# The first batch's attention output is split into the first token block's operands directly instead of through memory

## The chip, the core and the metric

The kernel runs on one core of one Trainium2 chip. The metric is the device time of one execution in microseconds (us). The kernel before takes 888.13 us, the median of three runs (887.55 to 888.17).

A core has five engines that run their own instruction streams and wait for one another by semaphores: TensorE (PE; matrix products and transposes into PSUM, PEld is its weight load), VectorE (DVE), ScalarE (ACT), GpSimd (POOL) and SyncE (SP), which here issues most of the DMAs.

## The reference

All arrays are fp32. `q`, `k` and `v` are 4 batches x 8 heads x 576 tokens x 64. The attention output becomes `x`, 2304 tokens x 512, and goes through two feed-forward stages:

```python
q_d, k_d, v_d = means over groups of 4 tokens          # 144 tokens per head
out_up = repeat(softmax(q_d k_d^T / 8) v_d, 4)          # pooled attention
mask = |i - j| < 4
out_local = softmax(where(mask, q k^T / 8, -1e6)) v     # local attention
x = (out_up + out_local) as (2304, 512)

h = x @ w_in                                            # 512 x 2048
x = (h * sigmoid(1.702 h)) @ w_out                      # 2048 x 512
y = ((x @ w1) * (x @ w2)) @ w3 @ w_out2                 # 512x1024, 512x1024, 1024x1024, 1024x512
```

## The kernel before

**Numbers.** A product in fp32 precision is made of three TensorE products (`mm3`, L117 to L120). Each operand is first split in two (`split`, L113): ScalarE copies it, rounded, into the high part `hi` (L114), and another engine subtracts that from the original to get the low part `lo` (L115). The weights come from memory in a packed form of two 32-bit words per number. Such a tile `st` of 512 KB is loaded, ScalarE makes `dec` from one word (L166), VectorE puts in the rest in three instructions (`decode`: L173, L176, L179), and then the tile is split into `w` (L184).

**Stage 0 (to about 120 us).** Nothing in the last two products lies between `w3` and `w_out2`, so they are folded into one matrix first, `w34 = w3 @ w_out2`, in 16 steps: 2 halves x 8 column tiles `j`. A step transposes a `w3` tile on TensorE (`w34_transpose`, L568, into `ps_w`, then split into `w3t`) and multiplies it (`w34_mm`, L578). After the eighth step of a half four results leave PSUM as `w34s` (L585, L586) and are written to memory. Between the products, `pump()` puts pieces of the first batch's attention: four head pairs, each with its transposes (`t_piece`, `qT` and `kT`, and the pooled `qd`, `kd`), local and pooled scores (`s_local` `ps_s`, `s_pool` `ps_sp`), softmax (`el`, `ep`), its transposes (`p_piece`, `ps_pt`) and values (`v_pool`, and `v_local` twice). The later `v_local` call of a pair covers the last 256 of the 576 tokens, the earlier one the first 320.

**How x gets to block 0.** `v_local` (L415 to L432) adds the local and the pooled part on VectorE into `xo` (L426) and writes it to the array `x_d` in memory (L430). When stage 0 is issued, `tok_load` (L593) loads 512 tokens of one head pair from there into `xr`, and `tok_split` (L598) splits it into `x_t`, for each of the four pairs (`kk`).

**Token blocks.** The feed-forward stage goes over blocks of 512, 512, 512, 256 and 512 tokens. In a block, step `f` of 16 makes 128 columns of `h` (`h_step`, L614: four `mm3`, one for each pair `kk`) and adds its share of `y` (`y_step`, L631); two `h` steps run ahead of their `y` step. The first block also carries the second batch's attention between its products, and the weights for each step are loaded, decoded and split just ahead of it.

**Memory on the chip.** Tiles live in pools with tags; a tile waits until an earlier tile of its tag is no longer read. The weight pool `wp` has 32 slots of tag "w". In `g2p` the tag "ys" has two slots, shared by `xo`, `w34s` and the block results. Staging tiles (`stage_tile`, L125) come from `stp` with three slots; in stage 0, four of each seven come from `xp`, whose four tags `x0` to `x3` later hold `x_t`.

**Order.** Each engine runs its instructions in one fixed order. The framework's scheduler makes it at build time, from the code's order, the dependencies and priorities (`decode` and the side work raise theirs). SyncE's DMA issues stand in such an order too: one that waits for its tile holds the ones behind it.

Of the kernel before, what the change touches and what calls it, by code (L numbers as in the profile page):

```python
# [10 lines left out]
F32R = mybir.dt.float32r  # L11
I32 = mybir.dt.int32
# [8 lines left out]
def fused_kernel(ctx, tc, q, k, v, w_in, w_out1, w1, w2, w3, w_out2, out):  # L21
    nc = tc.nc
    B, H, S, D = q.shape
# [6 lines left out]
    KD = DM // 128  # L30
# [4 lines left out]
    QB = 64  # L35
# [19 lines left out]
    NB = 512  # L55
# [9 lines left out]
    wp = ctx.enter_context(tc.tile_pool(name="wp", bufs=2 * NF))  # L65
    stp = ctx.enter_context(tc.tile_pool(name="stp", bufs=3))
    dp = ctx.enter_context(tc.tile_pool(name="dp", bufs=2))
    xp = ctx.enter_context(tc.tile_pool(name="xp", bufs=1))
# [10 lines left out]
    x_d = dram.tile([128, KD, NT], F32, name="x_d")  # L79
# [30 lines left out]
    def f32(ap):  # L110
        return ap.bitcast(F32)

    def split(raw, hi, lo, lo_eng):  # L113
        nc.scalar.activation(hi, raw, AF.Copy)  # L114
        lo_eng.tensor_tensor(lo, raw, f32(hi), op=ALU.subtract)  # L115
# [9 lines left out]
    def stage_tile(first):  # L125

        i = early["st"]
        early["st"] += 1
        if first and i % (3 + KD) >= 3:
            return xp.tile([128, 512, 2], I32, tag=f"x{i % (3 + KD) - 3}", name="st")  # L130
        return stp.tile([128, 512, 2], I32, tag="st", name="st")

    def decode_tile(first):
# [13 lines left out]
    def load_rows(w, f, first=False):  # L147
        st = stage_tile(first)
        nc.sync.dma_start(out=st.rearrange("p e w -> p (e w)"), in_=w.bitcast(I32)[f * 128:(f + 1) * 128, :])
        return st  # L150
# [73 lines left out]
            del self.decoded[:n]  # L224


    at = {}

    def head_ap(src, b, hp, tok, dims):
        off = ((b * H + 2 * hp) * S + tok) * D  # L230
# [184 lines left out]
    def v_local(n, i0, i1):  # L415
        vw, od = at["vw", n, i0 // HQ], at["od", n]
        xo = g2p.tile([128, NB], F32, tag="ys", name="xo")[:, :(i1 - i0) * QB]
        ps = pst.tile([128, (i1 - i0) * QB], F32, tag="t", name="ps_v")
        for i in range(i0, i1):
            for h in range(2):  # L420
                p = slice(h * D, (h + 1) * D)
                nc.tensor.matmul(
                    ps[p, (i - i0) * QB:(i - i0 + 1) * QB], vw[:, i - i0, h], at["PT", n, i // NPH][:, i % NPH, h * QB:(h + 1) * QB],
                    start=True, stop=True)
        u0, u1 = i0 * UB, i1 * UB
        nc.vector.tensor_tensor(  # L426
            xo.rearrange("p (u r) -> p u r", r=FAC), ps.rearrange("p (u r) -> p u r", r=FAC),
            od[:, u0:u1].unsqueeze(2).to_broadcast([128, u1 - u0, FAC]), op=ALU.add)
        b, hp = divmod(n, HP)
        nc.sync.dma_start(out=x_d[:, hp, b * S + i0 * QB:b * S + i1 * QB], in_=xo)  # L430
        if i1 == NQB and n + 1 < B * HP and n + 1 not in LOCAL:
            att_load_v(n + 1)  # L432

# [154 lines left out]
            pump()  # L588


    xh, xl, xr = {}, {}, {}

    def tok_load(src, j, kk):  # L593
        c0, n = BLOCKS[j]
        xr[j, kk] = t = g2p.tile([128, NB], F32, tag="xr", name="xr")
        nc.sync.dma_start(out=t[:, :n], in_=src[:, kk, c0:c0 + n])

    def tok_split(j, kk):  # L598
        n = BLOCKS[j][1]
        t = xr.pop((j, kk))  # L600
        x = xp.tile([128, 2, NB], F32R, tag=f"x{kk}", name="x_t")
        xh[kk], xl[kk] = x[:, 0], x[:, 1]
        split(t[:, :n], xh[kk][:, :n], xl[kk][:, :n], nc.vector)

    def tok_rest(src, j):
        for kk in range(KD):
            tok_split(j, kk)
            if kk + 2 < KD:
                tok_load(src, j, kk + 2)
# [172 lines left out]
    if True:  # L782
# [50 lines left out]
            jobs.size(njobs(s + 4))  # L833
        pump.drain()
        early["pri"] = 100
        tok_load(x_d, 0, 0)
        tok_load(x_d, 0, 1)
        jobs.split(2)
        tok_rest(x_d, 0)

        def w34_load(f):
            t = g2p.tile([128, NB], F32, tag="xr", name="w34r")
# [143 lines left out]
```

## Time and profile before

| | |
|---|---|
| median of three runs | 888.13 us |
| the profiled execution | 892.31 us |
| its span, first to last instruction | 890.5 us |
| TensorE busy, mean granted clock | 846.0 us (95%), 0.986 |
| VectorE busy | 589.5 us (66%) |
| ScalarE busy | 408.7 us (46%) |
| GpSimd busy | 150.6 us (17%) |
| bytes moved | 150.76 MB, 169 GB/s |

The profiled execution is one run with the profiler on; its span is 1.8 us shorter than its time. In the profile a line like `PE L118 MATMUL ps_h<-x_t,w` is an instruction of line 118 that writes the tile `ps_h` and reads `x_t` and `w`; `[0.63 <-DVE x_t L115]` behind it says that the engine was idle for 0.63 us before it, and what released it. PEclk is the granted TensorE clock as a share of full speed.

### The profile page before, as it was taken

How to read it: one execution, taken by the hardware profiler on the slowest of the kernel's cores; microseconds unless marked ns; L12 is line 12 of the kernel's file. 1: busy time of each engine (PE TensorE's matmuls, PEld its weight loads, DVE VectorE, ACT ScalarE, POOL GpSimd, SP SyncE). 2: the span in 40 equal slices, each digit the busy share in tenths (PEclk: the TensorE clock that was granted, in tenths of full speed). 3: DMA queues.
4: the chain of work that ended last, by engine and by line, in shares of the span. 5: the costliest groups of instructions: out<-in, count | busy, mean ns of one | idle time of the engine just before them, and what ended most of it. 6: DMA issues, size and time to landing. Idle time of an engine off the chain costs nothing.

```text
span 890.5 us, 13711 instructions
## 1 busy us (share of the span) xinstructions
PE 846.0 (95%) x5132; PEld 712.1 (80%) x5132; DVE 589.5 (66%) x1053; ACT 408.7 (46%) x862; POOL 150.6 (17%) x153
## 2 busy tenths in 40 slices
PE   5789979999999999999999999999999999999998
PEld 4567757666677777777789988889999899989996
DVE  5997587889998795847758973253456455555551
ACT  4667567567657665455446663342112211232111
POOL 7524241244332323311200000000000000000000
PEclk9799999999999999999999999999999999999999
DMA  8865584565656243553348989102556364635521
GB/s 239 270 207 160 155 249 129 163 182 170 158 156 123 63 108 87 131 126 62 78 148 304 358 325 348 49 1 86 210 196 259 105 244 166 255 135 222 191 84 71
DMA packets 140598, 150.76 MB, mean 169 GB/s; under 512 B 86898, under 2 KB 121460, under 8 KB 136436
## 3 DMA queue, kind: packets, MB, share of 16 engines
q1 hardware_dynamic: 119424, 141.21, 49.1%
q10 hardware_dynamic: 21108, 8.69, 4.0%
q8 instruction: 40, 0.66, 0.3%
q14 instruction: 26, 0.21, 0.1%
HBM read 117.75 MB, written 32.11 MB: 168 GB/s over the span
## 4 chain that ended last, share of the span: by engine, by line
PE 72%; DVE 12%; DMA 7%; issue 3%; ACT 3%; POOL 2%; ACTq 0%; SPq 0%; DVEq 0%; POOLq 0%
PE ps_ab L120 7%; PE ps_ab L118 7%; PE ps_ab L119 7%; PE ps_h L118 6%; PE ps_y L118 5%; PE ps_y L120 5%; PE ps_h L119 5%; PE ps_y L119 5%; PE ps_h L120 5%; PE ps_o L120 4%; PE ps_o L119 4%; PE ps_o L118 4%; DMA st<-in_moe_w_in_dram 3%; DVE dec L179 2%; DVE st L176 2%
## 5 line engine op out<-in xcount | busy, mean ns | idle before, releaser
L118 PE MATMUL ps_h<-x_t,w 128*128 128x512 f32 (+1 forms) x320 | 122.7, 385 | 3.0 <-DVE w L115 2.0
L118 PE MATMUL ps_y<-gh,w 128*128 128x512 f32 (+1 forms) x320 | 122.5, 383 | 0.0
L119 PE MATMUL ps_h<-x_t,w 128*128 128x512 f32 (+1 forms) x320 | 119.2, 372 | 1.1 <-DVE x_t L115 1.1
L119 PE MATMUL ps_y<-gl,w 128*128 128x512 f32 (+1 forms) x320 | 118.8, 371 | 0.4 <-DVE gl L115 0.4
L120 PE MATMUL ps_y<-gh,w 128*128 128x512 f32 (+1 forms) x320 | 119.2, 372 | 0.0
L120 PE MATMUL ps_h<-x_t,w 128*128 128x512 f32 (+1 forms) x320 | 118.5, 370 | 0.0
L120 PE MATMUL ps_ab<-b_t,a_in 128*128 128x384 f32 x336 | 112.5, 335 | 0.0
L118 PE MATMUL ps_ab<-b_t,a_in 128*128 128x384 f32 x336 | 112.5, 335 | 0.0
L119 PE MATMUL ps_ab<-b_t,a_in 128*128 128x384 f32 x336 | 112.4, 334 | 0.0
L115 DVE TENSOR_TENSOR gl<-g_t,gh 128x512 fp32r<-128x512 f32 (+1 forms) x80 | 55.0, 690 | 65.8 <-ACT gh L114 65.5
L624 ACT ACTIVATE g_t<-ps_h 128x512 f32<-128x512 f32 (+1 forms) x80 | 44.3, 555 | 92.0 <-PE ps_h L120 87.9
L114 ACT ACTIVATE abh<-ab 128x384 fp32r<-128x384 f32 x24 | 12.7, 527 | 137.5 <-DVE ab L749 137.5
L118 PEld LDWEIGHTS ps_h<-x_t,w 128*128 128x128 f32 x320 | 60.5, 190 | 17.2 <-DVE w L115 3.7
L118 PEld LDWEIGHTS ps_y<-gh,w 128*128 128x128 f32 x320 | 60.5, 189 | 11.8 <-issue 2.4
L119 PEld LDWEIGHTS ps_h<-x_t,w 128*128 128x128 f32 x320 | 60.8, 190 | 11.0 <-DVE x_t L115 2.2
L120 PEld LDWEIGHTS ps_y<-gh,w 128*128 128x128 f32 x320 | 60.5, 189 | 10.4
L120 PEld LDWEIGHTS ps_h<-x_t,w 128*128 128x128 f32 x320 | 60.5, 189 | 10.4 <-issue 0.2
L119 PEld LDWEIGHTS ps_y<-gl,w 128*128 128x128 f32 x320 | 60.6, 189 | 9.3 <-DVE gl L115 0.5
L118 PEld LDWEIGHTS ps_ab<-b_t,a_in 128*128 128x128 f32 x336 | 63.1, 188 | 0.9
L119 PEld LDWEIGHTS ps_ab<-b_t,a_in 128*128 128x128 f32 x336 | 63.1, 188 | 0.9
L179 DVE SCALAR_TENSOR_TENSOR dec<-dec,st 128x512 int32<-128x512 int32 x72 | 59.3, 833 | 6.0 <-ACT dec L166 4.8
L120 PEld LDWEIGHTS ps_ab<-b_t,a_in 128*128 128x128 f32 x336 | 63.1, 188 | 0.0
(150 smaller groups left out, 1667.3 us busy)
## 6 DMA issues: line engine op xcount, KB each, us to landing
a_in<-a_d SPq DMA_DIRECT2D x24, 1792.0 KB
st<-in_moe_w_dram SPq DMA_DIRECT2D x32, 512.0 KB
a_d<-ap SPq DMA_DIRECT2D x8, 1792.0 KB
st<-in_moe_w_out_dram SPq DMA_DIRECT2D x24, 512.0 KB
st<-in_moe_w_in_dram SPq DMA_DIRECT2D x16, 512.0 KB
yr<-y_d SPq DMA_DIRECT2D x12, 384.0 KB
out_dram<-osb SPq DMA_DIRECT2D x17, 256.0 KB
s_v<-in_v_dram ACTq DMA_DIRECT2D x15, 288.0 KB
```

Source lines behind the costliest of these rows:

```text
L114: nc.scalar.activation(hi, raw, AF.Copy)
L115: lo_eng.tensor_tensor(lo, raw, f32(hi), op=ALU.subtract)
L118: nc.tensor.matmul(ps, ll, rh, start=start, stop=False, skip_group_check=more)
L119: nc.tensor.matmul(ps, lh, rl, start=False, stop=False, skip_group_check=more)
L120: nc.tensor.matmul(ps, lh, rh, start=False, stop=stop, skip_group_check=more)
L176: nc.vector.scalar_tensor_tensor(low, st[:, :, 1], -0x80000000, low, op0=ALU.bitwise_and, op1=ALU.bitwise_or)
L179: nc.vector.scalar_tensor_tensor(t, t, 3, st[:, :, 0], op0=ALU.logical_shift_left, op1=ALU.bitwise_or)
L624: nc.scalar.activation(g[:, :n], ps[:, :n], AF.Gelu_apprx_sigmoid)
```

## The change

`v_local` for the first batch allocates the pair's `x_t` at its first call and splits `xo` straight into it, in pieces of 320 and 192 tokens. Only the tokens from 512 on (64 a pair) are still written to `x_d`. The loads and splits of the first block go. As the tiles `x0` to `x3` now hold `x` during stage 0, the staging tiles that were there come from the weight pool.

```diff
--- before.py
+++ after.py
@@ -127,7 +127,7 @@
         i = early["st"]
         early["st"] += 1
         if first and i % (3 + KD) >= 3:
-            return xp.tile([128, 512, 2], I32, tag=f"x{i % (3 + KD) - 3}", name="st")
+            return wp.tile([128, 512, 2], I32, tag="w", name="st")
         return stp.tile([128, 512, 2], I32, tag="st", name="st")
 
     def decode_tile(first):
@@ -224,7 +224,7 @@
             del self.decoded[:n]
 
 
-    at = {}
+    at, xh, xl = {}, {}, {}
 
     def head_ap(src, b, hp, tok, dims):
         off = ((b * H + 2 * hp) * S + tok) * D
@@ -427,7 +427,17 @@
             xo.rearrange("p (u r) -> p u r", r=FAC), ps.rearrange("p (u r) -> p u r", r=FAC),
             od[:, u0:u1].unsqueeze(2).to_broadcast([128, u1 - u0, FAC]), op=ALU.add)
         b, hp = divmod(n, HP)
-        nc.sync.dma_start(out=x_d[:, hp, b * S + i0 * QB:b * S + i1 * QB], in_=xo)
+        t0, t1 = b * S + i0 * QB, b * S + i1 * QB
+        if b == 0:
+
+            if hp not in xh:
+                x = xp.tile([128, 2, NB], F32R, tag=f"x{hp}", name="x_t")
+                xh[hp], xl[hp] = x[:, 0], x[:, 1]
+            c = slice(t0, min(t1, NB))
+            split(xo[:, :c.stop - t0], xh[hp][:, c], xl[hp][:, c], nc.vector)
+        m = max(t0, NB) if b == 0 else t0
+        if m < t1:
+            nc.sync.dma_start(out=x_d[:, hp, m:t1], in_=xo[:, m - t0:])
         if i1 == NQB and n + 1 < B * HP and n + 1 not in LOCAL:
             att_load_v(n + 1)
 
@@ -588,7 +598,7 @@
             pump()
 
 
-    xh, xl, xr = {}, {}, {}
+    xr = {}
 
     def tok_load(src, j, kk):
         c0, n = BLOCKS[j]
@@ -833,10 +843,7 @@
             jobs.size(njobs(s + 4))
         pump.drain()
         early["pri"] = 100
-        tok_load(x_d, 0, 0)
-        tok_load(x_d, 0, 1)
         jobs.split(2)
-        tok_rest(x_d, 0)
 
         def w34_load(f):
             t = g2p.tile([128, NB], F32, tag="xr", name="w34r")
```

The change also moves instructions. In the rows below a number behind a name tells tiles of one name apart.

TensorE where block 0 begins, before: `ps_h_1459` and `ps_h_1514` are `h` tiles of the first steps, `x_t_1435` and `x_t_1438` the x of the third and the last pair; `ps_t`, `ps_s` and `ps_sp` belong to the second batch's first pair.

```order
L284 MATMUL ps_t_1522<-ident_96,s_k_1049 128x72 x4
L118 MATMUL ps_h_1514<-x_t_1435,w_1441 128x512
L119 MATMUL ps_h_1514<-x_t_1435,w_1441 128x512
L120 MATMUL ps_h_1514<-x_t_1435,w_1441 128x512
L284 MATMUL ps_t_1540<-ident_96,s_k_1049 128x72 x4
L333 MATMUL ps_s_1601<-kT_1521,qT_1466 64x72 x10
L333 MATMUL ps_s_1622<-kT_1521,qT_1466 64x72 x8
L352 MATMUL ps_sp_1666<-kd_1546,qd_99 64x144 x6
L118 MATMUL ps_h_1459<-x_t_1438,w_1419 128x512
L118 MATMUL ps_h_1514<-x_t_1438,w_1441 128x512
L119 MATMUL ps_h_1459<-x_t_1438,w_1419 128x512
L120 MATMUL ps_h_1459<-x_t_1438,w_1419 128x512
```

The same place after: `ps_h_1455` and `ps_h_1510` are the first two `h` tiles, and `x_t_1208` and `x_t_1357` the third and the last pair's x (`x_t_657` and `x_t_948` the first two).

```order
L119 MATMUL ps_h_1455<-x_t_1208,w_1431 128x512
L120 MATMUL ps_h_1455<-x_t_1208,w_1431 128x512
L118 MATMUL ps_h_1455<-x_t_1357,w_1431 128x512
L284 MATMUL ps_t_1481<-ident_96,s_q_1054 128x72 x4
L118 MATMUL ps_h_1510<-x_t_657,w_1437 128x512
L119 MATMUL ps_h_1510<-x_t_657,w_1437 128x512
L120 MATMUL ps_h_1510<-x_t_657,w_1437 128x512
L119 MATMUL ps_h_1455<-x_t_1357,w_1431 128x512
L120 MATMUL ps_h_1455<-x_t_1357,w_1431 128x512
L118 MATMUL ps_h_1510<-x_t_948,w_1437 128x512
L119 MATMUL ps_h_1510<-x_t_948,w_1437 128x512
L120 MATMUL ps_h_1510<-x_t_948,w_1437 128x512
```

The second batch's scores `ps_s` and `ps_sp` stood ahead of the last pair's products of the first two `h` tiles; they now stand further back, the pooled ones behind 54 products of block 0. The first `h` tile is finished for all four pairs ahead of them, and the last pair's x is asked for earlier in the block.

VectorE at the same place, before: `st_1453` and `dec_1500` are a weight being decoded, the tiles `w` are weights being split.

```order
L173 TENSOR_SCALAR st_1453<-st_1453 128x512
L115 TENSOR_TENSOR x_t_1435<-xr_1428,x_t_1435 128x512
L176 SCALAR_TENSOR_TENSOR st_1453<-st_1453 128x512
L115 TENSOR_TENSOR w_1444<-dec_1378,w_1444 128x512
L115 TENSOR_TENSOR w_1494<-dec_1411,w_1494 128x512
L115 TENSOR_TENSOR w_1497<-dec_1413,w_1497 128x512
L179 SCALAR_TENSOR_TENSOR dec_1500<-dec_1500,st_1453 128x512
L336 TENSOR_TENSOR el_1597<-ps_s_1601,band_97 128x360
L115 TENSOR_TENSOR w_1550<-dec_1500,w_1550 128x512
L337 TENSOR_REDUCE mx_1599<-el_1597 128x5
L115 TENSOR_TENSOR x_t_1438<-xr_1433,x_t_1438 128x512
```

After: `xo_1344` and `xo_1363` are the last pair's output, `st_1449` and `st_1451` the fourth staging tiles of `w_in` and `w_out`.

```order
L115 TENSOR_TENSOR w_1431<-dec_1280,w_1431 128x512
L115 TENSOR_TENSOR w_1434<-dec_1282,w_1434 128x512
L426 TENSOR_TENSOR xo_1344<-ps_v_1345,od_1339 128x320
L426 TENSOR_TENSOR xo_1363<-ps_v_1364,od_1339 128x256
L115 TENSOR_TENSOR w_1437<-dec_1327,w_1437 128x512
L173 TENSOR_SCALAR st_1449<-st_1449 128x512
L115 TENSOR_TENSOR x_t_1357<-xo_1344,x_t_1357 128x320
L176 SCALAR_TENSOR_TENSOR st_1449<-st_1449 128x512
L173 TENSOR_SCALAR st_1451<-st_1451 128x512
L179 SCALAR_TENSOR_TENSOR dec_1496<-dec_1496,st_1449 128x512
L176 SCALAR_TENSOR_TENSOR st_1451<-st_1451 128x512
L115 TENSOR_TENSOR x_t_1357<-xo_1363,x_t_1357 128x192
```

The last pair's two `xo` and its two subtracts into `x_t_1357` now stand in one row with the decodes of `st_1449` and `st_1451`; the later subtract is behind the first instructions of both.

SyncE in the first part of stage 0, before: `st` are the staged `w3` tiles, `vw` the value windows of the second head pair, `xo` the first pair's output.

```order
L154 DMA st_815<-in_moe2_w3_dram 128x4x256
L154 DMA st_917<-in_moe2_w3_dram 128x4x256
L154 DMA st_998<-in_moe2_w3_dram 128x4x256
L154 DMA st_1066<-in_moe2_w3_dram 128x4x256
L154 DMA st_1145<-in_moe2_w3_dram 128x4x256
L267 DMA vw_673<-in_v_dram 72x2x64
L430 DMA x_d_92<-xo_644 128x320
L271 DMA vw_673<-in_v_dram 72x4x64 x2
L430 DMA x_d_92<-xo_661 128x256
L271 DMA vw_677<-in_v_dram 72x3x64 x2
L267 DMA vw_677<-in_v_dram 72x2x64
```

After:

```order
L154 DMA st_756<-in_moe2_w3_dram 128x4x256
L154 DMA st_1074<-in_moe2_w3_dram 128x4x256
L267 DMA vw_677<-in_v_dram 72x2x64
L271 DMA vw_677<-in_v_dram 72x4x64
L440 DMA x_d_92<-xo_663 128x64
L271 DMA vw_677<-in_v_dram 72x4x64
L271 DMA vw_681<-in_v_dram 72x3x64 x2
L267 DMA vw_681<-in_v_dram 72x2x64
L154 DMA st_819<-in_moe2_w3_dram 128x4x256
L154 DMA st_1153<-in_moe2_w3_dram 128x4x256
L154 DMA st_921<-in_moe2_w3_dram 128x4x256
```

The last three `w3` loads (`st_819`, `st_1153`, `st_921`) stood ahead of the second pair's window loads and now stand behind them; of the two writes of `xo` one small one is left.

## Rows read from the trace of the kernel before

**Rows 1.** Stretches: start:end, length, each engine's busy time (count), clock, DMA share, GB/s.
```profile
53.00:120.00 67.00, 63.64 (x569) 49.11 (x570) 50.61 (x94) 44.52 (x134) 25.75 (x27) 0.95 0.63 182
120.00:134.00 14.00, 9.23 (x85) 7.28 (x84) 11.33 (x20) 7.65 (x13) 6.29 (x7) 0.92 0.91 271
134.00:222.00 88.00, 81.34 (x526) 60.78 (x526) 75.84 (x122) 59.42 (x99) 27.50 (x28) 0.99 0.55 161
222.00:890.00 668.00, 659.85 (x3778) 570.52 (x3776) 410.38 (x758) 268.18 (x552) 60.34 (x44) 1.00 0.50 162
```

**Rows 2.** TensorE's waits, 0 to 120 us: us in total, times, longest.
```profile
PE ps_w L573 <- DVE dec L179: 16.4, 4, 9.0
```

**Rows 3.** TensorE's timeline, 88 to 134 us: start, busy, instruction [idle before <-releaser].
```profile
90.05 0.47 PE L284 MATMUL ps_t<-ident,s_k 72*128 72x72 f32 x4 [1.66 <-DVE xo L426]
...
116.22 0.75 PE L422 MATMUL ps_v<-PT,vw 72*64 72x64 f32 x20
...
117.33 0.69 PE L422 MATMUL ps_v<-PT,vw 72*64 72x64 f32 x16
...
120.14 0.39 PE L118 MATMUL ps_h<-x_t,w 128*128 128x512 f32 x1
120.37 0.39 PE L119 MATMUL ps_h<-x_t,w 128*128 128x512 f32 x1
...
121.51 0.42 PE L284 MATMUL ps_t<-ident,s_q 72*128 72x72 f32 x4
...
122.90 0.50 PE L119 MATMUL ps_h<-x_t,w 128*128 128x512 f32 x1 [0.63 <-DVE x_t L115]
...
126.96 1.37 PE L333 MATMUL ps_s<-kT,qT 64*64 64x72 f32 x36 [0.47 <-ACT kT L285]
132.01 1.70 PE L352 MATMUL ps_sp<-kd,qd 64*64 64x144 f32 x12 [3.68 <-POOL kd L296]
```

**Rows 4.** VectorE's timeline, 60 to 125 us.
```profile
74.75 0.69 DVE L179 SCALAR_TENSOR_TENSOR dec<-dec,st 128x512 int32<-128x512 int32 x1 [0.38 <-ACT dec L166]
...
88.25 0.43 DVE L173 TENSOR_SCALAR st<-st 128x512 int32<-128x512 int32 x1 [3.03 <-DMA st<-in_moe_w_in_dram]
...
117.75 1.28 DVE L115 TENSOR_TENSOR w<-dec,w 128x512 fp32r<-128x512 f32 x2
118.96 0.48 DVE L426 TENSOR_TENSOR xo<-ps_v,od 128x320 f32<-128x320 f32 x1
```

**Rows 5.** GpSimd's timeline, around 130 us.
```profile
130.18 1.78 POOL L296 TENSOR_TENSOR kd<-kd,kT 128x144 f32<-128x144 f32 x2
```

**Rows 6.** ScalarE's timeline, around 124 us.
```profile
123.13 1.13 ACT L586 ACTIVATE w34s<-ps_w 128x512 f32<-128x512 f32 x2 [3.39 <-DMA x_d<-xo]
...
124.16 1.20 ACT L285 ACTIVATE qT<-ps_t 128x288 f32<-128x288 f32 x2
```

**Rows 7.** Two short stretches, columns as in rows 1.
```profile
88.00:95.00 7.00, 5.34 (x29) 4.20 (x27) 3.06 (x5) 2.18 (x4) 5.22 (x7) 0.76 0.59 168
...
131.00:137.00 6.00, 4.99 (x25) 3.91 (x26) 3.57 (x8) 1.55 (x4) 0.88 (x2) 0.72 0.66 211
```

**Rows 8.** The splits of x: count, ns min/median/max, first and last start, shapes.
```profile
L114 ACT ACTIVATE x_t<-xr x20: 399/631/637, 103.1 to 527.7; 128x512 fp32r<-128x512 f32 x16, 128x256 fp32r<-128x256 f32 x4
L115 DVE TENSOR_TENSOR x_t<-xr,x_t x20: 418/684/1783, 107.7 to 528.4; 128x512 fp32r<-128x512 f32 x16, 128x256 fp32r<-128x256 f32 x4
```

**Rows 9.** SyncE's timeline, around 66 us (SPq: its DMA queue).
```profile
66.35 0.44 SPq L267 DMA_DIRECT2D vw<-in_v_dram  x1
```

**Rows 10.** Chain of waits, 85 to 200 us: start, us, what.
```profile
102.83 4.40 DMA st<-in_moe_w_in_dram
...
140.61 5.03 DMA st<-in_moe_w_out_dram
...
160.40 6.25 DMA st<-in_moe_w_in_dram
```

**Rows 11.** TensorE's waits, 133 to 260 us, columns as in rows 2.
```profile
PE ps_h L118 <- DVE w L115: 2.0, 3, 0.8
```

## The prediction

> **What bounds the kernel now.** I read the stretches first, with the busy time of each engine. From 222 us on TensorE is busy 659.85 of 668 us, and the change moves nothing there. Between 53 and 120 us (the fold of w3 into w_out2, with the first batch's attention between its products) it is busy 63.64 of 67, at a granted clock of 0.95; between 120 and 134 us, where the first token block begins, only 9.23 of 14, at 0.92 [rows 1]. So in the middle of the kernel time is TensorE's time, and a change is worth the TensorE idle time that it removes or makes.
>
> Next I read what TensorE waited for. Up to 120 us the large item is 16.4 us in four waits of the w3 transposes for VectorE's decode [rows 2]; all four end by 54 us. In the timeline of TensorE two places are left. At 90.05 it resumes after 1.66 us for an `xo`, whose VectorE instruction stood behind a decode that had waited 3.03 us for a weight load [rows 3, 4]. And at the head of block 0 it waits 0.63 for an x split, 0.47 for `kT` and 3.68 for `kd` [rows 3].
>
> The last is the longest, and its cause is not where it shows. `kd` is summed on GpSimd up to 131.96 [rows 5]. That waited for `qT`, which ScalarE copied only from 124.16, because the `w34s` copy ahead of it sat 3.39 us, to 123.13, for the write of `xo` to memory [rows 6]: `w34s` and `xo` share two slots. The round trip of x itself costs TensorE only 0.63 us.
>
> An idle stretch also costs clock: between 88 and 95 us the granted clock is 0.76, between 131 and 137 it is 0.72 [rows 7], which is the 1.2 GHz level for part of each. 7 x 0.24 = 1.7 and 6 x 0.28 = 1.7; since the means also cover part of the idle time I take 1.5 us for each.
>
> **Removed.** Eight writes of the first batch's `xo` shrink to four of 64 columns, and four loads of x go. That frees the two shared slots: `w34s` now waits for the split that reads `xo` (for the second slot also for a small write). The four full splits go, each 0.63 us on ScalarE and 0.68 on VectorE [rows 8]. Neither engine is what TensorE waits for there; TensorE loses no instruction.
>
> **Moved.** In the changed order the pooled scores `ps_sp` of the second batch stand 54 products behind the start of block 0 (all of the first three h tiles, the first y step and half an h tile) instead of 18, at 0.23 us a product [rows 3]. So the waits for `kT` and `kd` (4.15 us) go, and so does the one for x of the third pair. At stake there: 0.63 + 0.47 + 3.68 + 1.5 of clock = 6.3 us. Late next on TensorE is x of the last pair, priced below.
>
> At 90 us the second pair's later `xo` now stands ahead of the decode that waits for a load. I let that stall go: 1.66 + 1.5 = 3.2 us (bounds: 0, if another wait takes its place, and 3.2).
>
> At the start, the first 12 fold products move behind the second w3 transposes. At most they cost 12 x 0.43 = 5.2 us at the low clock (an estimate, twice the row's 0.23); the cover is the 16.4 us that TensorE waits for decodes before 54 us anyway, and VectorE has the same decodes to make by then. I cost it at nothing. Without the cover the 5.2 us would be paid in full.
>
> The new staging tiles sit in the weight pool, which has 32 slots. The first stage allocates 8 + 16 + 12 = 36, and by the time a slot comes round its old tile (a staging tile, a w3 tile or a w_out2 tile used in an earlier step) has been read: nothing.
>
> **Added.** Eight smaller splits. From 399 and 631 ns for 256 and 512 columns on ScalarE, and 418 and 684 on VectorE [rows 8], a 320-column piece is about 0.46 and 0.49 us and a 192-column piece 0.34 and 0.35: together 3.2 and 3.4 us against 2.5 and 2.7 removed. Between 53 and 120 us VectorE has 16 and ScalarE 22 us free [rows 1]: hidden, but for the last pair.
>
> The last pair's second subtract stands on VectorE behind the decode of two weights whose loads need slots that VectorE itself frees only just before. In the old kernel's times: the pair's first `xo` starts at 118.96, and in the changed order one small subtract, two decodes and two weight splits lie between it and the release of the first slot. At 0.6 us for a full operation [rows 4], that release is at 118.96 - 0.3 - 1.2 - 1.2 = 116.25. One issue takes 0.4 [rows 9] and I take 5.03 for the load [rows 10]: it lands at 121.7. VectorE is there at 118.96 + 0.4 + 0.35 + 0.6 = 120.3 and waits 1.4. Then 0.4 + 0.45 + 0.6 to 123.15; the second load, released 0.9 later, has landed (122.6); then 0.4 + 0.6 + 0.6 + 0.3 to 125.05, and x is complete.
>
> TensorE wants it after the pair's first value products (end 116.97): the second value products 0.6, 19 products at 0.23 and two groups of transposes at 0.23 each [rows 3], that is at 122.4. It waits 2.6 us. Bounds: with loads of 4.40 and 6.25 us [rows 10] 2.0 and 3.8; if VectorE is 2 us less behind than it was, 0.6. To this comes 0 to 1.5 us of clock; I take 2.6 + 1.5 = 4.1.
>
> By the Trainium skill ("DMA: Bandwidth & Descriptors", "Anatomy of one DMA"), fitted on the GpSimd path, a transfer takes about 2.0 us plus its bytes at 436 GB/s; that would be an estimated 3.2 us for these 512 KB, x would be complete with the decodes alone, and the sum 1.4 us better. The rows disagree (4.40 to 6.25), and the rows decide. In the other direction the skill ("SBUF — State Buffer", "SBUF: two separate sides") says that a VectorE operation with two SBUF inputs and a GpSimd operation that reads SBUF exclude each other. The new subtracts are of that kind; the row's longest x split, 1783 ns against a median of 684, fits it. By this rule the third pair's two subtracts, beside GpSimd's scaling, could each lose up to 1.1 us, and the wait would be up to 2.2 us longer.
>
> **Sum.** 6.3 + 3.2 - 4.1 = 5.4 us. The profiled execution took 892.31 us (span 890.5 and 1.8 around it), which becomes 886.9; the median of the timed runs is 888.13, 0.9953 of it, so I predict 882.8 us. By the bounds: 9.5 - 0.6 = 8.9 us gained at best (879.3), and at worst 6.3 - 5.3 = 1.0 (887.1).
>
> **Rivals.**
> 1. The new wait for x eats the gain. For it: one product on TensorE stands behind a chain of two loads, three copies on ScalarE and ten VectorE instructions. Against it: it must reach 3.8 us with the full clock loss, and the stall at 90 us must stay. Then 6.3 - 5.3 = 1.0 us: 887.1, which is no change.
> 2. Block 0 is fed by weights, and gives the gain back. For it: TensorE already waits for a weight three times between 133 and 260 us, 2.0 us together [rows 11]. Against it: VectorE is busy 75.84 of 88 us after 134 [rows 1], and the loads of the fourth weight pair now stand ahead of the fold's stores on SyncE. To keep pace VectorE must take 5.4 us out of its 12.2 free; if it manages half, 2.7 us stay: 885.4.
> 3. Slower. The last three w3 loads now stand on SyncE behind the window loads of the second pair, issued only when the first pair's value products free their tile, to 66.8 us [rows 9]. Their decodes stand ahead of the one that at 74.75 gave TensorE its next tile [rows 4]. With 6.25 us for the first and 2.9 for each further one (512 KB at the stretch's 182 GB/s [rows 1]) they land at 73.0, 75.9 and 78.8; the second makes that decode start at 77.1, 2.3 late, the third holds the score chain 2.3 more; 1.5 of clock, and the later `xo` brings the 3.2 at 90 us back as paid, not gained. 2.3 + 2.3 + 1.5 = 6.1, against 6.3 - 4.1 = 2.2 that remain: 3.9 us slower, 892.0. It decides from a second landing after about 74 us. Against it: at 5.03 us and less crowding the second lands near 73.
>
> **Chances.** Forecast 0.64, nearly all of it faster; weights 0.12, of which 0.08 faster and 0.04 no change; x wait 0.12 (0.02 faster, 0.08 none, 0.02 slower); late w3 loads 0.12, slower by all but 0.01. About 0.2%, 1.8 us, is what a measurement can tell. Faster: 0.62 + 0.08 + 0.02 = 0.72; none: 0.02 + 0.04 + 0.08 + 0.01 = 0.15; slower 0.13. The forecast's own range is 879.3 to 887.1; 8 in 10 with the first two rivals: 879.3 to 888.3.
>
> **What would show it.** In the new profile `w34s` no longer waits on a write of `xo` at the head of block 0; `ps_sp` there waits for nothing; one product of the first h tile waits 1 to 4 us for the VectorE split of x, behind decodes that wait for loads; no wait for `xo` near 90 us; the order is that of before from about 168 us, and everything there comes about 5 us earlier. It is wrong if a new wait over 2 us stands between 53 and 120 us, if the w waits in block 0 grow by what was gained, or if TensorE reaches the fold's middle (about 54 us) more than 2 us late.

## The result and the profile after

The changed kernel is slower. Its first four runs had a median of 894.69 us against 888.15 us before, a ratio of 1.0073 (95% interval 1.0051 to 1.0096). Measured again with more runs beside each other it was 894.14 against 889.68, 1.0054 (1.0030 to 1.0079): 4.8 us, between 2.7 and 7.0. The prediction was 882.8 us, and its range ended at 888.3.

Two things must be known to read the traces. The kernel before varies more than its first three runs told: 29 runs lay between 885.7 and 894.1 us. And one profiled execution is one draw of these, so I compare two traces of each kernel where I have them (the second of before is experiment e0, of after f1). In e1, e3, f2, f3, f4 and g1 the profiled execution was the fastest of its group and in e2 the slowest, so a single trace tells which waits are there better than what a kernel takes. The ratios leave out two single executions, 4510.86 us in f3 and 2100.57 us in l2, far outside their groups. The stretches end at marks that each kernel has: ScalarE's copy of the pooled values `od` of the first batch's first pair, of its last pair, and the eighth `h` tile of block 0 (`g_t`).

Stretches of the kernel before, second trace (columns as in [rows 1]):

```profile
0.00:62.41 62.41, 40.85 (x253) 31.08 (x254) 49.99 (x76) 33.24 (x80) 33.38 (x51) 0.89 0.80 238
62.41:118.03 55.62, 52.52 (x471) 40.38 (x469) 40.08 (x76) 37.45 (x115) 22.19 (x25) 0.97 0.59 165
118.03:183.24 65.21, 58.46 (x405) 44.90 (x401) 57.01 (x93) 44.04 (x76) 19.35 (x21) 0.97 0.62 185
```

The same stretches of the changed kernel:

```profile
0.00:63.72 63.72, 40.20 (x253) 30.66 (x254) 49.93 (x74) 32.36 (x81) 33.47 (x51) 0.87 0.73 208
63.72:124.02 60.30, 53.83 (x465) 41.18 (x465) 44.76 (x86) 39.24 (x120) 20.98 (x24) 0.94 0.60 163
124.02:187.26 63.24, 57.98 (x412) 44.20 (x407) 50.98 (x89) 42.98 (x74) 19.68 (x21) 0.97 0.57 172
```

With the other trace of each (before: 61.33, 55.47, 67.21; after: 64.53, 60.00, 63.07) the means are 61.9, 55.5 and 66.2 us before and 64.1, 60.2 and 63.2 after. So the changed kernel loses 2.2 us up to the first pair's values, loses 4.6 us in the rest of the fold, and wins 3.0 us where block 0 begins. What follows lasts 705.1 us before (the two traces differ by 2.8) and 704.9 after: there is nothing in it, as the prediction said. The sum is 3.6 us slower by the traces, 4.8 by the times.

**The first loss** begins with a wait that the kernel before does not have. TensorE's timeline after:

```profile
13.62 2.42 PE L333 MATMUL ps_s<-kT,qT 64*64 64x72 f32 x36 [0.73 <-ACT kT L285]
...
21.30 0.74 PE L284 MATMUL ps_t<-ident,s_q 72*128 72x72 f32 x4 [3.95 <-DVE el L336]
```

The same place in the second trace of before, where 12 fold products fill the time in which the scores and transposes find their operands:

```profile
11.85 0.78 PE L118 MATMUL ps_w<-w,w3t 128*128 128x512 f32 x1
...
17.26 0.59 PE L120 MATMUL ps_w<-w,w3t 128*128 128x512 f32 x1
17.78 1.35 PE L333 MATMUL ps_s<-kT,qT 64*64 64x72 f32 x36
```

After, those products stand behind the scores, and TensorE idles 3.95 us for `el`. But that hole is made up: with the same 36 fold products done, TensorE reaches its fifth group of w3 transposes at 39.22 us here and at 39.52 in f1, against 39.70 and 40.76 in the two traces of before. The time is lost behind it. TensorE after:

```profile
39.22 1.12 PE L583 MATMUL ps_w<-ident,dec 128*128 128x128 f32 x4 [2.56 <-DVE dec L179]
...
51.89 0.50 PE L118 MATMUL ps_w<-w,w3t 128*128 128x512 f32 x1 [2.66 <-DVE w3t L585]
```

Second trace of before:

```profile
40.76 0.66 PE L573 MATMUL ps_w<-ident,dec 128*128 128x128 f32 x4 [3.90 <-DVE dec L179]
...
49.55 0.50 PE L118 MATMUL ps_w<-w,w3t 128*128 128x512 f32 x1 [0.72 <-DVE w3t L575]
```

Eight transposes of `el` that stood ahead of the decode wait before (at 35.80 us) now stand behind it (41.82 and 43.40). And VectorE's split of `w3t` at 51.16 has nine decode instructions since the split before it, where both traces of before have seven: TensorE waits 2.66 us for it (2.99 in f1), where it waited 0.41 and 0.72. The second pair's scores then start 2.3 us late by the means. No run separates these two from each other.

**The second loss** is on SyncE. Its timeline after (`st<-in_moe_w_dram` are the w3 loads, seven in the first line and three in the last):

```profile
35.65 25.16 SPq L154 DMA_DIRECT2D st<-in_moe_w_dram  x7
65.22 0.33 SPq L267 DMA_DIRECT2D vw<-in_v_dram  x1
...
69.47 0.40 SPq L267 DMA_DIRECT2D vw<-in_v_dram  x1
69.92 3.23 SPq L154 DMA_DIRECT2D st<-in_moe_w_dram  x3
```

VectorE after, which decodes what lands:

```profile
76.22 0.61 DVE L173 TENSOR_SCALAR st<-st 128x512 int32<-128x512 int32 x1 [2.49 <-DMA st<-in_moe_w_dram]
...
79.06 0.43 DVE L173 TENSOR_SCALAR st<-st 128x512 int32<-128x512 int32 x1 [1.50 <-DMA st<-in_moe_w_dram]
...
95.74 0.42 DVE L426 TENSOR_TENSOR xo<-ps_v,od 128x256 f32<-128x256 f32 x1 [1.71 <-DMA w_d<-w34s]
```

The last three w3 loads are issued behind the window loads `vw`, at 69.92 to 73.15. The first of the three follows the last window load (69.47 and 0.40 us) at once, so no slot held it, only its place in the order; the third is issued at 72.78, after 1.9 us that the profile puts down to a window load. VectorE waits 2.49 us to 76.22 and 1.50 us to 79.06 for them; in [rows 4] it was past that point at 74.75. In f1 the profile's chain puts the wait that ends at 79.57 down to the second of the three, issued at 71.22. The third line: near 95 us `xo` now waits for a write of `w34s`, the same sharing of two slots the other way round. This is the profile's reading in one trace only; in f1, where the wait is 2.23 us, it names a window load. TensorE's stall there, 1.66 us in [rows 3], is still 1.07 and 0.67 us in the two traces. TensorE's longest waits in the rest of this stretch, after:

```profile
77.28 0.52 PE L395 MATMUL ps_pt<-ident,ep 128*72 128x128 f32 x3 [1.99 <-ACT PT L396]
...
82.01 1.71 PE L352 MATMUL ps_sp<-kd,qd 64*64 64x144 f32 x12 [1.61 <-DVE el L336]
...
118.53 0.60 PE L395 MATMUL ps_pt<-ident,el 128*72 128x128 f32 x4 [1.15 <-DVE xo L426]
```

Before, the first was 1.05 and 0.29 us, and the other two were not there. Not all of this comes from the late loads: e3, below, has its loads early and still waits 1.65 us for `el` at 77.77.

**The gain** is where the prediction put it. ScalarE at the head of block 0, after:

```profile
127.53 0.59 ACT L596 ACTIVATE w34s<-ps_w 128x512 f32<-128x512 f32 x1
128.55 0.70 ACT L285 ACTIVATE qT<-ps_t 128x288 f32<-128x288 f32 x1 [0.43 <-PE ps_t L284]
```

`w34s` waits for no write, where it sat 3.39 us in [rows 6], and `qT` is no longer held by it. The waits of 0.63, 0.47 and 3.68 us of [rows 3] are gone. New ones stand further on. TensorE after (the first row is a product that needs the last pair's x complete):

```profile
130.32 0.40 PE L119 MATMUL ps_h<-x_t,w 128*128 128x512 f32 x1
...
139.57 0.63 PE L119 MATMUL ps_y<-gl,w 128*128 128x512 f32 x1 [2.94 <-DVE gl L115]
...
164.74 1.07 PE L395 MATMUL ps_pt<-ident,el 128*72 128x128 f32 x8 [2.22 <-POOL el L375]
```

The wait for `gl` is one for a weight: VectorE makes `gl` at 138.84, behind a decode that waited for its load.

```profile
138.18 0.73 DVE L173 TENSOR_SCALAR st<-st 128x512 int32<-128x512 int32 x1 [5.30 <-DMA st<-in_moe_w_in_dram]
```

### The profile page after: what moved, and what is told of

It is laid out like the page before. It is cut to its first block, busy times and chain, and to the rows that moved or that the text cites. A ratio compares the mean times of both kernels' runs of the same rounds, so it can differ in the third digit from the quotient of the medians.

```text
span 892.0 us, 13691 instructions
## 1 busy us (share of the span) xinstructions
PE 845.4 (95%) x5132; PEld 711.0 (80%) x5132; DVE 589.1 (66%) x1057; ACT 407.8 (46%) x866; POOL 149.3 (17%) x153
## 4 chain that ended last, share of the span: by engine, by line
PE 74%; DVE 12%; DMA 7%; ACT 3%; issue 2%; POOL 1%; ACTq 1%; SPq 0%; DVEq 0%
PE ps_ab L120 7%; PE ps_ab L118 7%; PE ps_ab L119 7%; PE ps_y L118 6%; PE ps_y L120 6%; PE ps_y L119 6%; PE ps_h L118 6%; PE ps_h L119 5%; PE ps_h L120 5%; PE ps_o L119 4%; PE ps_o L120 4%; PE ps_o L118 4%; DVE dec L179 3%; PE ps_pt L395 2%; DVE st L176 2%
## 5 line engine op out<-in xcount | busy, mean ns | idle before, releaser
L115 DVE TENSOR_TENSOR gl<-g_t,gh 128x512 fp32r<-128x512 f32 (+1 forms) x80 | 55.5, 695 | 65.6 <-ACT gh L114 65.0
L120 PEld LDWEIGHTS ps_y<-gh,w 128*128 128x128 f32 x320 | 60.5, 189 | 10.4
L179 DVE SCALAR_TENSOR_TENSOR dec<-dec,st 128x512 int32<-128x512 int32 x72 | 56.7, 796 | 3.1 <-ACT dec L166 2.0
```

Source lines behind the costliest of these rows:

```text
L120: nc.tensor.matmul(ps, lh, rh, start=False, stop=stop, skip_group_check=more)
L179: nc.vector.scalar_tensor_tensor(t, t, 3, st[:, :, 0], op0=ALU.logical_shift_left, op1=ALU.bitwise_or)
```

## The experiments

Ratios are to the kernel before, run beside each kernel, with 95% intervals. **e0: the kernel before again.**

> The kernel before, unchanged, for a second trace. Its profiled execution was 892.31 us where the timed runs were 888.15, so 4.2 us of that trace may belong to that one execution. If the trace was typical, TensorE again waits 3.7 us for kd at the head of block 0 and 1.7 us for xo near 90 us, and only the rest of the execution is shorter. If it was a bad execution, one or both waits are under 1 us, and the 6.3 and 3.2 us that the prediction counted on were not there to be had in most executions.

Ratio 1.0006 (0.9981 to 1.0031). This execution took 888.64 us, 3.7 less than the first trace, and the waits are there again: 3.55 us for `kd`, 1.67 for `xo`. So they belong to the kernel, and the 4.2 us by which the first trace stood above the median do not come from them. (For the wait of `w34s`, 3.13 us here, this profile names a split of x and not the write of `xo`; f4 tests that cause.)

**e1: the staging tiles alone.** x goes through memory as before.

```diff
-            return xp.tile([128, 512, 2], I32, tag=f"x{i % (3 + KD) - 3}", name="st")
+            return wp.tile([128, 512, 2], I32, tag="w", name="st")
```

> The staging half of the change alone: the staging tiles come from the weight pool, x still goes through memory. Theory 1 (the staging tiles cost the time: their loads stand late on SyncE and the first fold products stand late on TensorE): the fold ends 6 to 8 us later than before, the w3 loads land near 76 and 79 us as in the changed kernel, and the time is 893 to 899. Rival A (the direct split costs the time, by its small splits and the xo slots held longer): the fold ends where it did, 887 to 889.

Ratio 1.0092 (1.0069 to 1.0116), 8.2 us slower. Its stretches:

```profile
0.00:64.53 64.53, 40.70 (x253) 30.93 (x254) 50.27 (x74) 32.07 (x81) 33.80 (x51) 0.87 0.73 209
64.53:124.83 60.30, 53.59 (x466) 40.75 (x466) 46.58 (x88) 39.73 (x119) 22.15 (x24) 0.97 0.73 206
124.83:190.46 65.63, 60.08 (x408) 46.08 (x403) 51.18 (x85) 42.49 (x72) 18.79 (x21) 0.90 0.54 155
```

Both losses are there in full (64.53 and 60.30), the gain is not (65.63). Theory 1 holds; rival A, that the splits cost the time, falls.

**e2: the direct split alone,** as near as it can be had (one staging tile of the third round uses the ordinary slots).

```diff
+            t = (0, 1, 2, 3, 0, 1, 2, 3, 1, 2, 3, None)[i // (3 + KD) * KD + i % (3 + KD) - 3]
+            if t is not None:
+                return xp.tile([128, 512, 2], I32, tag=f"x{t}", name="st")
```

> The direct split alone, as near as it can be had: the staging tiles stay in x0 to x3 for the first two rounds, and in the third round three of them use x1 to x3 and the fourth the ordinary staging slots, so that x0 is free for the first pair's x. Theory 1: the order of the early fold is that of before, the fold ends within 1 us of before, and the head of block 0 gives back what the prediction said: 882 to 885. Rival A (the direct split costs the time): 893 to 896. Rival B (the direct split gives nothing, because the kd wait turns into another): 887 to 889.

Ratio 1.0010 (0.9990 to 1.0031): rival B's number. The fold is near that of before (62.48 and 57.06 us), and so is the third stretch (66.53): the split alone does not gain the 3 to 6 us that theory 1 forecast.

**e3 and g0: the changed kernel with the order repaired.** It keeps both halves of the change; the staging tiles are only written once at the start.

```diff
+    ahead = [wp.tile([128, 512, 2], I32, tag="w", name="st") for _ in range(12)]
+    for t in ahead:
+        nc.gpsimd.memset(t[:1, 0, :1], 0)
...
-            return wp.tile([128, 512, 2], I32, tag="w", name="st")
+            return ahead.pop(0)
```

> The changed kernel, whose twelve staging tiles from the weight pool are each written once by a tiny memset on GpSimd at the very start, so that they have their slots before any weight asks for one. The loads of w3 then stand on SyncE in the order of before, ahead of the window loads, and the first fold products stand where they did. Theory 1 (order is what the staging tiles changed, not a real wait for a slot): no VectorE wait over 1 us for a w3 load near 76 us, 882 to 885. Rival C (sharing the weight pool costs by itself, by real waits for slots or by traffic): 891 to 895 as the changed kernel.

> The changed kernel with all twelve staging tiles given their slots at the start, once more, beside the next two: 0.9991 of before with an interval of 0.26% to either side. If the direct split gives what its removed waits lasted, 0.3 to 0.6% faster than before must show in the two measurements together; if block 0 gives it back, within 0.2%.

Ratios 0.9991 (0.9965 to 1.0017) and 0.9974 (0.9952 to 0.9997). SyncE in e3:

```profile
36.74 23.29 SPq L157 DMA_DIRECT2D st<-in_moe_w_dram  x9
63.21 0.33 SPq L270 DMA_DIRECT2D vw<-in_v_dram  x1
```

All nine loads are out by 60 us, ahead of the windows. The stretches of e3:

```profile
0.00:61.47 61.47, 39.97 (x252) 30.39 (x253) 49.35 (x76) 33.30 (x81) 35.29 (x63) 0.89 0.80 242
61.47:116.14 54.67, 51.58 (x468) 39.69 (x466) 40.69 (x80) 37.88 (x118) 20.58 (x25) 0.97 0.49 134
116.14:180.61 64.47, 58.50 (x407) 44.34 (x403) 56.07 (x93) 44.04 (x77) 20.19 (x21) 1.00 0.62 182
```

Both losses are gone here (61.47 and 54.67), with the same tiles in the same pool. In g0 the first is gone (60.88); the middle stretch is 58.09, at a mean clock of 0.91, with TensorE busy 54.19 us where e3's is busy 51.58. So what cost the time was the order and not the sharing of the pool. What fits is that in one tag the scheduler grants slots in the order of first writes, so that a staging tile's load stands behind the weight splits and `w3t` tiles that the code writes before it, and that an early write sets it free; no run shows this rule itself. Against the kernel before the repaired version is 0.8 and 2.3 us faster, where the second interval leaves out 1 and the first doesn't: hardly a gain. e3's trace, 885.24 us, flatters it. In g0 (888.10, median 887.62) the eighth `h` tile stands at 183.32, against 184.01 and 183.24 before.

**f1: the changed kernel again** (the numbers stand above).

> The changed kernel again, beside the others, since 25 runs of the kernel before lay between 885.5 and 894.9 and the first comparison had four of each. By the first comparison 0.7% slower, near 897 beside a kernel before at 890.5; if those four were chance, within 0.3% of before.

**f2 and f3: half the repair each**, the early write for the last four staging tiles only, and for the first eight only.

> The changed kernel, with only the last four staging tiles given their slots at the start: on SyncE the last w3 loads stand ahead of the window loads again, while the first fold products stay behind the scores. Theory 1 with late loads as the larger half: the stretch from the first to the last head pair's pooled values is back at 55 us (60.3 in the changed kernel), the stretch before it stays at 64 (before 61 to 62): 0.2% slower than before. Theory 1 with the early order as the larger half: the later stretch stays near 60, 0.5 to 0.7% slower.

> The other half: only the first eight staging tiles have their slots at the start, so that the first fold products stand where they did, and the last w3 loads stay behind the window loads. If the late loads are the larger half: the first stretch is back at 61 to 62 us, the second stays near 60, 0.4 to 0.6% slower than before. If the early order is the larger half: 0.2% slower or less.

f2: 1.0064 (1.0040 to 1.0089). f3: 1.0046 (1.0024 to 1.0067). The stretches of f2:

```profile
0.00:62.72 62.72, 40.42 (x249) 31.16 (x250) 49.43 (x76) 31.31 (x73) 34.03 (x54) 0.92 0.81 228
62.72:119.19 56.47, 50.34 (x460) 39.02 (x461) 40.48 (x79) 37.82 (x124) 22.26 (x25) 1.00 0.50 137
119.19:188.13 68.94, 60.66 (x421) 45.83 (x415) 54.82 (x95) 44.90 (x76) 21.58 (x21) 0.98 0.60 173
```

And of f3:

```profile
0.00:61.85 61.85, 40.22 (x253) 30.79 (x254) 47.95 (x75) 33.28 (x81) 35.25 (x59) 0.89 0.73 215
61.85:120.99 59.14, 54.50 (x464) 41.96 (x465) 43.08 (x86) 39.03 (x120) 20.54 (x24) 0.94 0.60 162
120.99:184.30 63.31, 59.36 (x412) 45.06 (x407) 52.90 (x89) 42.81 (x74) 18.70 (x21) 0.95 0.57 175
```

The middle stretch follows the late loads as expected: 56.47 us with them repaired, 59.14 with them late. The first follows the early order (61.85 where it is repaired; f2's 62.72 is between). But neither half is worth its share in time. f2 loses 2.7 us at the head instead of winning 3.0 (68.94 against 66.2); TensorE waits there 2.42 us for an `xo` at 128.40, among others. For f3 the three stretches give 0.7 us slower where the times say 4.1; its profiled execution, 890.14 us, was the fastest of its runs, so the size of this half stays open.

**f4: only the shared slots.** x through memory, `w34s` in the unused slots of tag g.

```diff
-                sb = g2p.tile([128, NB], F32, tag="ys", name="w34s")
+                sb = g2p.tile([128, NB], F32, tag="g", name="w34s")
```

> The kernel before, x through memory, with w34s in the two slots of tag g, which stage 0 does not use, instead of those of xo. The prediction said that the 3.7 us wait for kd at the head of block 0 comes from that sharing. If so and if the wait is worth what it lasts, w34s waits for no write of xo, the kd wait is under 1 us, and the kernel is 0.4 to 0.6% faster. If the wait goes and the time is given back (block 0 is held by its weights or by the second batch's softmax), the wait is gone and the time is within 0.2% of before. If the cause is another, the wait stays.

Ratio 1.0011 (0.9987 to 1.0035). ScalarE and TensorE in f4:

```profile
123.76 0.60 ACT L586 ACTIVATE w34s<-ps_w 128x512 f32<-128x512 f32 x1 [0.29 <-DMA w_d<-w34s]
```

```profile
127.55 0.95 PE L352 MATMUL ps_sp<-kd,qd 64*64 64x144 f32 x12 [1.73 <-POOL kd L296]
```

The cause was read rightly: the copy's wait is 0.29 us and the `kd` wait half of what it was (the first two copies also moved forward, to 114.25 and 116.95 us). But the time is the same: the interval leaves room for 1.2 us gained. A wait of 2 us that goes at the head of block 0 is not 2 us less.

**What takes the gain back.** In e3 TensorE waits again at the end of the second batch's softmax:

```profile
141.25 0.47 PE L287 MATMUL ps_t<-ident,s_q 72*128 72x72 f32 x4 [0.98 <-DVE el L339]
...
157.41 1.07 PE L398 MATMUL ps_pt<-ident,el 128*72 128x128 f32 x8 [2.80 <-POOL el L378]
```

VectorE's and GpSimd's part in it:

```profile
145.23 0.60 DVE L357 TENSOR_REDUCE mx<-ps_sp 128x3 f32<-128x432 f32 x1
...
155.17 0.22 DVE L375 RECIPROCAL sm<-sm 128x12 f32<-128x12 f32 x1
```

```profile
155.64 1.71 POOL L378 TENSOR_TENSOR el<-el,sm 128x648 f32<-128x648 f32 x1
```

TensorE made the pooled scores that the row at 145.23 reads from 137.73 on. VectorE comes to them only then, and to the reciprocal ten microseconds later, in between decodes and splits of weights; then GpSimd scales `el`. TensorE, now earlier, waits for that. Not all of it is new: before, TensorE waited 3.5 and 2.3 us in that place for copies and a weight. From the last pooled values to the eighth `h` tile its waits add up to 8.3 and 6.5 us in the two traces of before, to 5.8 in e3 and 4.7 in g0. Three pairs of runs were to tell what block 0 follows.

g1 and g2: the low part of each `w_out` tile subtracted on GpSimd, in the kernel before and in e3.

```diff
-            jobs.append((("wo1", f), lambda f=f: load_rows(w_out1, f), nc.vector, f < 3))
+            jobs.append((("wo1", f), lambda f=f: load_rows(w_out1, f), nc.gpsimd, f < 3))
```

> The kernel before with one of five VectorE instructions taken off every w_out tile of the first feed-forward layer: its low part is subtracted on GpSimd. TensorE's order is that of before. Of VectorE's 75.8 us between 134 and 222 us some ten times 0.8, 8 us, go. Theory 2 (block 0 follows VectorE, which decodes its weights): 0.3 to 0.6% faster than before. Rival D (block 0 does not follow VectorE, but the loads' latency through three staging slots, or TensorE itself): within 0.2%; slower if GpSimd's longer instruction makes the weights later.

> The same edit in the changed kernel with the staging tiles' slots given at the start, again with TensorE's order unchanged. Theory 2: the waits that the direct split removes at the head of block 0 now pay, since VectorE keeps pace: faster than the kernel before by 0.6 to 1.0%, and by 0.3% or more than the same edit in the kernel before. Rival D: the same gain or none in both, so that the direct split gives nothing here either.

1.0162 (1.0129 to 1.0195) and 1.0123 (1.0088 to 1.0159). GpSimd's instruction in g1, 134 to 222 us (count, busy us, mean ns, idle before):

```profile
L115 POOL TENSOR_TENSOR w<-dec,w 128x512 fp32r<-128x512 f32 x9 | 13.3, 1482 | 35.1 <-ACT w L114 35.1
```

It takes 1.48 us where VectorE took 0.83 and 0.93 in the two traces of before, and both kernels lose 11 to 14 us. But g1 does not test a less busy VectorE. Its trace has 16 VectorE instructions fewer (1037 against 1053) and the same busy time, 590.2 us against 589.5 and 591.8, as others became longer: L173 took 0.64 us in the same window, against 0.49 and 0.54. So theory 2 is neither shown nor refuted here, and that the later weights cost the time is only argued.

k1 and k2: a fourth staging slot, in the kernel before and in e3.

```diff
-    stp = ctx.enter_context(tc.tile_pool(name="stp", bufs=3))
+    stp = ctx.enter_context(tc.tile_pool(name="stp", bufs=4))
...
-                if key[0] not in ("wo2", "w3") and len(self.loaded) + len(self.sized) >= 3:
+                if key[0] not in ("wo2", "w3") and len(self.loaded) + len(self.sized) >= 4:
...
-        xr[j, kk] = t = g2p.tile([128, NB], F32, tag="xr", name="xr")
+        xr[j, kk] = t = g2p.tile([128, NB], F32, tag="g", name="xr")
```

> The kernel before with a fourth staging slot for weights, and four instead of three weights allowed between load and decode. Its 4 KB come from the two slots of tag xr, whose users share tag g instead. Theory 3 (block 0 follows the weights' round trip of load, decode and release through three slots): VectorE's waits for weight loads between 134 and 222 us (8 to 9 us in the kernel before) shrink to under 4, the stretch after the last pooled values of the first batch falls from 55 to 57 us to 53 or less, 0.3 to 0.6% faster than before. Rival E (block 0 follows TensorE's own order and the softmax chain): within 0.2%, whatever the loads do; slower if the shared tag g makes block results wait.

> The same edit in the changed kernel with the staging tiles' slots given at the start. Theory 3: the waits removed at the head of block 0 pay now, faster than before by 0.6 to 1.0%, and by 0.3% or more than the same edit in the kernel before. Rival E: as without the edit, 0.1 to 0.3% faster than before, so the head's gain is lost to something other than the weight loads.

1.0355 (1.0311 to 1.0400) and 1.0291 (1.0259 to 1.0323). Not conclusive: the shared tag g makes later blocks wait for x (10.4 and 8.6 us after 250 us), which hides the question. VectorE's waits for weight loads between 134 and 222 us did not shrink (10.4 us in k1, 13.8 in k2, 8.4 in e0), so theory 3 has nothing for it.

l1 and l2: the sign bits of all weights decoded after the fold left out, in the kernel before and in e3.

```diff
-            for st, t in sts:
+            for st, t in sts if early["pri"] == 200 else []:
                 low = st[:, :, 0]
                 nc.vector.scalar_tensor_tensor(
                     low, st[:, :, 1], -0x80000000, low, op0=ALU.bitwise_and, op1=ALU.bitwise_or)
```

> The kernel before without the instruction that brings the sign bit into a decoded weight, for all weights decoded after the fold, so they come out positive: one of five VectorE instructions of 0.72 us on every weight, some 19 of them (13.6 us of VectorE's 75.8) between 134 and 222 us. Orders of TensorE are unchanged. Theory F (block 0 follows VectorE, in whose queue both the weights and the second batch's softmax stand): the stretch from the first batch's last pooled values to those of the second batch's first pair falls from 55 to 57 us by 2 or more, and the kernel is 0.3 to 0.8% faster. Rival E (TensorE's own order and fixed chains): within 0.2%.

> The same left out in the changed kernel with the staging tiles' slots given at the start. Theory F: the direct split's removed waits now pay, faster than before by 0.6 to 1.2%, and by 0.3% or more than the same in the kernel before; the wait of ps_pt for el near 157 us falls from 2.8 us to under 1.5. Rival E: the same 0.1 to 0.3% as without the edit, and the el wait stays.

0.9969 (0.9944 to 0.9994) and 1.0018 (0.9998 to 1.0038). Here VectorE is less busy (563.6 us in l1). The kernel before wins 2.8 us, and e3 nothing: in l2 the first `el` wait falls to 1.34 us as theory F forecast, a later one is 3.6, and the time does not follow. In the trace of l1 theory F's stretch is as forecast: from the first batch's last pooled values to the second batch's first it takes 51.8 us, where before it took 57.0 and 55.0. Its eighth `h` tile stands at 174.52 us, 9 us earlier than before, and most of that is given back behind it: what follows lasts 711.4 us instead of 705.1, and TensorE waits 4.71 us for a later pair's `el`:

```profile
212.06 1.92 PE L395 MATMUL ps_pt<-ident,el 128*72 128x128 f32 x8 [4.71 <-POOL el L375]
```

TensorE's order is not quite that of before in l1, though its expectation says so, so this can't be put down to VectorE alone. In l2 VectorE waits 20.6 us for weight loads between 116 and 222 us. So less work on VectorE goes with an earlier first half of block 0, but no single engine is shown to hold the whole of it: waits for the weights' loads, VectorE and the softmax chain are all in the traces, and which of them would have to go first stays open.

## Why the prediction was wrong

- **Staging tiles in the weight pool, "nothing".** This step failed, and cost most: alone it made the kernel 8.2 us slower (e1); in the changed kernel the stretch with the late loads is 4.6 us longer. I asked whether a slot would be held (the first late load was held by none) and not what the shared tag does to the order of the loads, though the changed SyncE order stood in front of me. It became rival 3, with 0.12. That rival's mechanism was right: w3 loads behind the windows hold VectorE's decodes. That its landings, 75.9 and 78.8, lie so near to 76.22 and 79.06 is partly luck: it meant the second and the third load, issued from 66.8; they were issued from 69.92, and f1's chain ends the later wait with the second. Its time, 892.0, was 3.9 us slower, and measured were 4.8; that is partly luck too, as it had nothing for the loss at the start.
- **The first 12 fold products, "at nothing".** Failed, by 2.2 us of its bound of 5.2 (the 0.43 in it is what the timelines show for a product there; twice 0.23 would be 0.46). The cover I named was TensorE's decode waits up to 54 us. It did repay the products, by 39 us. What it did not cover is what moved with them: eight transposes of `el`, and VectorE's order, in which a split of `w3t` now comes later and TensorE waits 2.66 us for it. I looked at what the moved products could be late for, and not at the rest of the order. The sign that I had named for it, the middle of the fold reached over 2 us late, came.
- **The stall at 90 us, 3.2 us.** Failed: 1.07 and 0.67 us are left. In one trace `xo` there waits for a write of `w34s`, in the other the profile names a window load, so the cause is not settled. If it is the first, I had read the sharing of the two slots at the head of block 0 and did not follow it to the other place where both are used. In e3 and g0, with the order repaired, this stall is gone, and e3's stretch is only 0.9 us shorter than before.
- **The head of block 0, 6.3 less 4.1.** The net was 2.2 and came out as 3.0, but by two errors that cancel, which is luck. The cause of the `kd` wait was right (f4, and the row of ScalarE), and its removal was worth less than it lasted. The wait for the last pair's x never came: the subtract starts at 129.51 and its product runs at 130.32 without a wait; in e3, where the fold is not late, TensorE does not wait for it either. What came were waits for `gl` (2.94), behind a weight's load as in rival 2, and for `el` (2.22).
- **The range.** It left rival 3 outside. Two unknown costs were set to zero, and their bounds (5.2 us for the start, 6.1 for the late loads) belonged into it. And 0.2% as what a measurement can tell rested on three runs within 0.6 us; groups of 4 to 29 runs of the kernel before had medians from 888.15 to 891.26.
- **Right:** nothing moves behind block 0 (705.1 and 704.9 us). The Trainium skill's rule ("SBUF — State Buffer", "SBUF: two separate sides"), that a VectorE operation with two SBUF inputs and a GpSimd operation that reads SBUF exclude each other, was to cost the third pair's subtracts up to 1.1 us each. The trace agrees for the first of them, 0.8 us longer than its like (0.48); it ended 0.35 us after GpSimd did. VectorE and GpSimd after:

```profile
119.55 1.25 DVE L115 TENSOR_TENSOR x_t<-xo,x_t 128x320 fp32r<-128x320 f32 x1
...
129.51 0.34 DVE L115 TENSOR_TENSOR x_t<-xo,x_t 128x192 fp32r<-128x192 f32 x1
```

```profile
118.71 1.74 POOL L300 TENSOR_TENSOR s_v<-s_v 72x512 f32<-72x512 f32 x1
```

## What to carry to other kernels

When a tile moves into a pool that others share, ask two questions: does it wait for a slot, and what does it now stand behind. In this kernel a shared pool put the loads into another order although the first late load waited for no slot, and a tiny early write set them free. And a wait on the busiest engine is worth what it lasts only if the next thing on that engine is ready; read who is late next for the whole stretch, not for one instruction.

## What the runs showed of the hardware

One program on one core varied by almost 1% (885.7 to 894.1 us in 29 runs). A 128x512 subtraction that took VectorE 0.83 and 0.93 us between 134 and 222 us took GpSimd 1.48 us, and with 16 of them moved there VectorE's busy time stayed the same (590.2 us against 589.5 and 591.8). Of three 512 KB loads issued behind each other, the second landed 8.33 us after its issue by the profile's chain (f1).
